# Six shared 8 KB places for transposed x and streamed weight blocks

## The chip, the core and the metric

The kernel runs on one core of one Trainium2 chip. The metric is the time of one execution on the device in microseconds (us). In three timed runs the kernel before took 891.34, 892.9 and 893.55 us, so its median is 892.9 us. All data are 32-bit floats. "PE" is the matrix engine, "DVE" the vector engine, "ACT" the scalar engine, "POOL" the GpSimd engine, and "SP" the sync engine, which here only issues DMA transfers.

## The reference

The reference is linear attention without a softmax, followed by a two-layer network with a squared ReLU:

```python
kv = np.einsum('bhsd,bhse->bhde', k, v)            # batch 8, heads 8, sequence 576, head 64
out = np.einsum('bhsd,bhde->bhse', q, kv)
rms = np.sqrt(np.mean(out * out, axis=-1, keepdims=True) + 1e-06)
attn = out / rms * g_norm
x = attn.transpose(0, 2, 1, 3).reshape(B * S, H * D)   # 4608 tokens x 512
h = x @ w_in                                        # 512 x 2048
g = np.maximum(h, 0.0) ** 2
result = g @ w_out                                  # 2048 x 512
```

## The kernel before, in words

The 4608 tokens are cut into nine strips of 512. For each strip the kernel first does the "up" product with w_in, then the "down" product with w_out. Both use a fast scheme of the Strassen kind: a product of 2 x 2 blocks is made of seven products p = 1 to 7 and of sums before and after. The down product of strips 1 to 8 applies it at two levels ("deep"), the up product does so from strip 2 on. So a strip's deep down stage has seven products p, in the order 4, 1, 2, 6, 5, 7, 3 (`DEEP_ORDER`, k = 0 to 6), and each of them has seven small products j. Product p is done in two halves, i = 0 with j = 1, 2, 3 and i = 1 with j = 4, 5, 6, 7. One small product is four 32-bit matmuls of 128 x 128 by 128 x 128, which the trace shows as eight records.

The weights of the deep stages don't all stay on the chip. They are summed once in strips 0 and 1, written to DRAM (`w_deep`, `w_in_deep`, `w_out`) and streamed back in every strip as blocks: each half product needs one, of 768 KB for i = 0 and 1 MB for i = 1, and each up product of a deep strip one of 768 KB. `stream()` (line 921) asks for the next block of a fixed list: it takes a place of 8 KB per partition from the pool `stream`, which has four, and lets SP issue the load. A place is free again when the last matmul that reads its block is done. From strip 2 on every call follows directly on the work that frees a place, so that four blocks are held or in flight at all times.

The same pool also lends places in strips 0 and 1 to the sums that are written to DRAM: `w_t` in `store_deep_sums` (line 951; `reserve`, line 918, takes the place earlier) and `w_i` in `deep_sums_in` (line 1146). The transposed x of a strip, `xT`, fills another 8 KB. It has a pool of its own with two places (line 86), one for the strip at work and one for the next, whose four tiles of 128 tokens arrive one after the other. Tiles of strip 0, of strip 1 and the first of strip 2 (tile 8) are transposed on PE and copied into place by ACT (`features`, line 627). All others are transposed in squares by DVE, written to DRAM (`send_x`, line 646) and fetched back by four transfers of 64 KB each (`fetch_x`, line 651). A fetch is due some units of a clock of steps after the send: 18 units for strip 2, 6 for later strips, where a step of strip 1 counts 2.2 in the up stage and 3.2 in the down stage.

The order of the work is written out by hand: within each engine instructions run in the order in which the program emits them. SP is one such queue. When a load waits for a place or for data, everything behind it waits too: x tiles, queries, keys, values, and stores of results. Attention is a list of `slices`, of which the main loop (line 298) puts a few between the steps of a strip. In strip 1 that list starts with the last odd tile of batch 1 and has `features` of tile 8 between the transposes T(2, 2) and T(2, 3), which DVE does.

In the down stage of strip 0 (one level, order 1, 2, 5, 6, 7, 3, 4) the loop asks for two blocks when the stage begins, for a third after p = 2 and for a fourth at its seventh step, and makes the deep sums of each block of weights soon after its product (`deep_due`, line 1402).

At the very end, product p = 3 of strip 8 is done in the second half of k = 6 in the groups of j (1), (2, 6, 5, 7) and (4, 3). After each group `together` (line 1058) does what it can of the sums on ACT and DVE into a tile `o` of 128 x 512, whose four quarters are numbered 0 to 3. The small products of p = 5 and p = 3 accumulate in the same PSUM tiles, of which there are two. The last sum adds j = 3 and j = 4 to quarters 0 and 3 together, and then `send` (line 946) stores the whole tile, 256 KB, with one transfer.

## Time and profile before

| what | value |
|---|---|
| median of three timed runs | 892.9 us |
| the profiled execution | 889.28 us |
| its span, first to last instruction | 887.3 us |
| PE busy | 876.6 us, 99% |
| PE weight loads busy | 821.8 us, 93% |
| DVE busy | 721.4 us, 81% |
| ACT busy | 352.3 us, 40% |
| POOL busy | 307.3 us, 35% |
| DMA, mean over the span | 266 GB/s |
| granted PE clock | 1.000 |

The profiled execution is one run with its own time, which is 3.6 us under the median. Its span leaves out about 2 us around the program. Durations are taken from it, so sums are made against 889.28 us. A busy engine in this profile is one that has an instruction under way. "Idle before" names the time an engine stood still before an instruction, and the arrow names what ended it. SP counts as never busy, but its own waits are listed separately.

### The profile page before, as it was taken

What the parts mean: (1) busy time and instruction counts of PE and PEld (TensorE: products, weight loads), DVE (VectorE), ACT (ScalarE), POOL (GpSimd) and SP (SyncE); (2) the same over time, 40 slices, a digit from 0 to 9 for tenths busy, and PEclk for the clock granted to TensorE, in tenths of its full rate; (3) what the DMA queues carried; (4) which work ended last, traced back from release to release, by engine and by line L of the source; (5) the groups of instructions that cost most, each with busy time, mean ns of one, the idle gap of its engine ahead of it and who ended that gap; (6) DMA issues with size and microseconds to landing.
All of it is one profiled execution on the core that took longest, in us unless ns stands there. A gap on an engine that the chain in (4) does not pass through costs nothing.

```text
span 887.3 us, 20876 instructions
## 1 busy us (share of the span) xinstructions
PE 876.6 (99%) x8296; PEld 821.8 (93%) x8296; DVE 721.4 (81%) x1233; ACT 352.3 (40%) x806; POOL 307.3 (35%) x315
## 2 busy tenths in 40 slices
PE   8999999999999999999999999999999999999998
PEld 7445888889999999999999999999999999999998
DVE  4999998879768986798678966897888778876886
ACT  4898242320048303740365034902491147102710
POOL 0000005610558223731474045604470447044700
PEclk9999999999999999999999999999999999999999
DMA  9998997989999888979887988898658864884385
GB/s 314 315 316 251 304 366 234 273 305 328 327 232 262 297 309 249 237 269 331 238 222 250 321 268 247 251 307 285 211 166 309 297 181 171 309 291 155 137 313 180
DMA packets 169953, 235.73 MB, mean 266 GB/s; under 512 B 79488, under 2 KB 134272, under 8 KB 161536
## 3 DMA queue, kind: packets, MB, share of 16 engines
q1 hardware_dynamic: 169696, 234.40, 82.3%
q8 instruction: 65, 1.06, 0.5%
q14 instruction: 32, 0.26, 0.1%
q10 hardware_dynamic: 160, 0.00, 0.0%
HBM read 197.66 MB, written 36.70 MB: 264 GB/s over the span
## 4 chain that ended last, share of the span: by engine, by line
PE 82%; DVE 10%; DMA 3%; ACT 3%; issue 2%; SPq 0%; POOL 0%; DVEq 0%; POOLq 0%; ACTq 0%
PE ps_B L1052 22%; PE ps_A L1248 19%; PE ps_A L1052 16%; PE ps_B L1248 9%; PE ps_C L1248 5%; PE ps_A L835 4%; PE kv_ps L432 2%; PE x_ps L468 2%; DVE w_c L269 2%; PE ps_B L835 1%; DMA w_deep<-w_t 1%; DVE w_t L289 1%; DVE wt L289 1%; PE ps_C L835 1%; DVE w_c L263 1%
## 5 line engine op out<-in xcount | busy, mean ns | idle before, releaser
L1052 PE MATMUL ps_B<-w_blk,g_s 128*128 128x128 f32 x1024 | 126.1, 275 | 0.0
L1052 PEld LDWEIGHTS ps_B<-w_blk,g_s 128*128 128x128 f32 x1024 | 120.0, 192 | 0.1
L1248 PE MATMUL ps_A<-x_l,w_in 128*128 128x128 f32 x784 | 103.8, 275 | 0.3 <-ACT snap L1265 0.3
L1052 PE MATMUL ps_B<-w_blk,gt 128*128 128x128 f32 x768 | 97.5, 275 | 1.5 <-DMA w_blk<-w_out 1.5
L289 POOL TENSOR_TENSOR x_l<-xT 128x256 f32<-128x256 f32 x21 | 15.4, 734 | 238.6 <-PE ps_A L1052 187.9
L1248 PEld LDWEIGHTS ps_A<-x_l,w_in 128*128 128x128 f32 x784 | 95.4, 192 | 0.6 <-ACT snap L1265 0.5
L1052 PE MATMUL ps_A<-w_blk,g_s 128*128 128x128 f32 x768 | 93.6, 275 | 0.0
L1052 PEld LDWEIGHTS ps_B<-w_blk,gt 128*128 128x128 f32 x768 | 91.5, 192 | 1.7 <-DMA w_blk<-w_out 1.7
L1052 PEld LDWEIGHTS ps_A<-w_blk,g_s 128*128 128x128 f32 x768 | 89.6, 192 | 0.0
L1260 POOL TENSOR_TENSOR snap<-snap,gt 128x512 f32<-128x512 f32 x35 | 45.9, 1310 | 119.2 <-ACT snap L1265 103.7
L1265 ACT COPY snap<-ps_A 128x512 f32<-128x512 f32 x63 | 36.9, 585 | 109.5 <-PE ps_A L1248 96.2
L1198 ACT ACTIVATE gt<-gt 128x512 f32<-128x512 f32 x112 | 70.1, 626 | 12.8 <-DVE gt L1260 12.6
L1052 PE MATMUL ps_A<-w_blk,gt 128*128 128x128 f32 x576 | 72.2, 275 | 0.0
L1199 ACT ACTIVATE gt<-gt 128x512 f32<-128x512 f32 x112 | 70.7, 631 | 3.6
L1052 PEld LDWEIGHTS ps_A<-w_blk,gt 128*128 128x128 f32 x576 | 68.2, 192 | 0.0
L1067 DVE TENSOR_TENSOR o_sb<-o_sb,ps_B 128x256 f32<-128x256 f32 (+1 forms) x128 | 49.4, 386 | 19.2 <-ACT o_sb L1068 11.8
L1068 ACT COPY o_sb<-ps_A 128x128 f32<-128x128 f32 x24 | 6.4, 265 | 145.7 <-PE ps_A L1052 145.7
L1154 POOL TENSOR_TENSOR w_i<-w_in 128x512 f32<-128x512 f32 x7 | 10.7, 1524 | 148.1 <-DMA q<-in_q_dram 140.8
L289 DVE TENSOR_TENSOR gt<-gt 128x2048 f32<-128x2048 f32 (+1 forms) x29 | 59.7, 2063 | 0.0
L1260 POOL TENSOR_TENSOR gt<-gt,snap 128x512 f32<-128x512 f32 x42 | 52.4, 1277 | 17.6 <-DVE snap L1260 17.4
L1248 PE MATMUL ps_B<-x_l,w_blk 128*128 128x128 f32 x392 | 52.1, 276 | 0.0
L1248 PE MATMUL ps_A<-x_l,w_blk 128*128 128x128 f32 x392 | 51.9, 275 | 0.0
(183 smaller groups left out, 1835.0 us busy)
## 6 DMA issues: line engine op xcount, KB each, us to landing
w_blk<-w_deep SPq DMA_DIRECT2D x56, 1024.0 KB, 6.5
w_blk<-w_out SPq DMA_DIRECT2D x56, 768.0 KB, 6.0
w_blk<-w_in_deep SPq DMA_DIRECT2D x49, 768.0 KB, 5.5
raw<-in_moe_w_in_dram SPq DMA_DIRECT2D x16, 512.0 KB, 7.0
raw<-in_moe_w_out_dram SPq DMA_DIRECT2D x16, 512.0 KB, 5.8
k<-in_k_dram SPq DMA_DIRECT2D x29, 256.0 KB, 5.2
v<-in_v_dram SPq DMA_DIRECT2D x29, 256.0 KB, 5.4
x_d<-x_q SPq DMA_DIRECT2D x27, 256.0 KB, 5.4
```

The source lines that it names most:

```text
L269: yield nc.vector.scalar_tensor_tensor(out=ci, in0=high, scalar=-(2**30), in1=ci, op0=ALU.bitwise_and, op1=ALU.bitwise_or)
L289: eng.tensor_tensor(out=out, in0=a, in1=b, op=ALU.subtract)
L432: nc.tensor.matmul(ps[ts(h, D), i], lhsT=a, rhs=w, start=i == 0 and c == 0, stop=c == C, skip_group_check=True)
L468: nc.tensor.matmul(ps[half, r, i, ts(p, D)], lhsT=q[row, half], rhs=kvd[b, p][row, row], start=True, stop=True)
L835: nc.tensor.matmul(bank[BANK[p]][:, i, :], lhsT=lhsT(k), rhs=rhs(k), start=p in (1, 5, 2) and i == 0 and k == 0, stop=k == n - 1, skip_gro ...
L1052: nc.tensor.matmul(chain[c][x][:, i, :], lhsT=a[:, f, :], rhs=w[:, f, :], start=x not in opened[c] and f == 0, stop=f == FQ // 2 - 1, skip ...
L1067: add = lambda out, a, b: nc.vector.tensor_tensor(out=out, in0=a, in1=b, op=ALU.add)
L1198: nc.scalar.activation(o, o, AF.Relu)
L1199: nc.scalar.activation(o, o, AF.Square)
L1248: nc.tensor.matmul(ps[:, i, :], lhsT=w, rhs=rhs, start=j in (1, 2, 5) and i == 0, stop=True, skip_group_check=True)
L1260: add = lambda eng, out, a, b: eng.tensor_tensor(out=out, in0=a, in1=b, op=ALU.add)
L1265: nc.scalar.copy(t, ps)
```

## The change

One pool of six places holds the streamed blocks, the weight sums and the transposed x of strips 1 to 8. The x of strip 0 has a place of its own in the storage that is given back when the weights have been converted, and the new pool lies on that storage.

- `stream()` is called once more at the start of each deep down stage (k = 0, i = 0) and no longer at k = 6, i = 0. Within the stage each block is asked for one half product earlier, and the total is the same.
- In strip 0 three blocks are asked for at the start of the down stage, the fourth after p = 2, and the request at its seventh step goes. The deep sums of p = 5 come one step later, behind those of p = 6.
- Tiles of strip 2 are due for fetching 12 units after their send, not 18.
- `features` of tile 8 comes after T(2, 3), not before it.
- The last strip's p = 5 and p = 3 use three PSUM tiles: j = 3 has one for itself. The last groups of j are (1), (2, 6, 5, 7), (4), (3). Quarters 1 and 2 of the last tile are stored before j = 4 and j = 3 are added, quarter 3 after j = 4, quarter 0 after j = 3: four transfers of 64 KB, one of them issued by ACT, in place of one of 256 KB.

```diff
-    xt_pool = ctx.enter_context(tc.tile_pool(name="xt", bufs=2))
...
     conv = ExitStack()
+    xt_pool = conv.enter_context(tc.tile_pool(name="xt", bufs=1))
...
     def open_xt(s):
         if s not in xt:
-            xt[s] = xt_pool.tile([P, STRIP // SQ, NP, SQ], FP32, name="xT", tag="xT")
+            if s == 0:
+                xt[s] = xt_pool.tile([P, STRIP // SQ, NP, SQ], FP32, name="xT", tag="xT")
+            else:
+                t = stream_pool.tile([P, 4, FQ // 2, P], FP32, name="xT", tag="w_blk")
+                xt[s] = t.rearrange("p n f e -> p (n f e)").rearrange("p (a q t) -> p a q t", q=NP, t=SQ)
         return xt[s]
...
-        tiles_due.append((clock[0] + (6 if n >= DEEP_UP * NT + NT else 18), fetch_x, (n,)))
+        tiles_due.append((clock[0] + (6 if n >= DEEP_UP * NT + NT else 12), fetch_x, (n,)))
...
-    slices += [(T, (2, 2)), (features, (last[0],)), (T, (2, 3)), (K, (2, 2, 3))]
+    slices += [(T, (2, 2)), (T, (2, 3)), (features, (last[0],)), (K, (2, 2, 3))]
...
+    def send_quarter(s, th, eh, o, t, h, eng):
+        for part, at, rows in out_rows(NT * s + 2 * th):
+            if at.start <= t < at.stop:
+                eng.dma_start(
+                    out=rows[:, t - at.start, eh * DH + h * P : eh * DH + (h + 1) * P], in_=o[part, t, ts(h, P)]
+                )
...
-    LAST_PLACE = {1: (1, 0), 2: (0, 0), 6: (0, 1), 5: (0, 2), 7: (0, 3), 3: (1, 1), 4: (1, 2)}
+    LAST_PLACE = {1: (1, 0), 2: (0, 0), 6: (0, 1), 5: (0, 2), 7: (0, 3), 3: (2, 0), 4: (1, 1)}
...
-            chain[c] = [fpsum.tile([P, 4, P], FP32, name=f"ps_{c}", tag="f") for _ in range(2)]
+            n = 2 + (s == N_STRIP - 1 and p == 5)
+            chain[c] = [fpsum.tile([P, 4, P], FP32, name=f"ps_{c}", tag="f") for _ in range(n)]
...
+        if s == N_STRIP - 1 and p in (5, 3):
+            if p == 3:
+                for t, h, eng in ((0, 1, nc.sync), (1, 0, nc.scalar)):
+                    send_quarter(s, 0, 1, o, t, h, eng)
+            yield
+            for j, t, h in ((4, 1, 1), (3, 0, 0)):
+                add(q[:, 2 * t + h], q[:, 2 * t + h], small(j)[:, 0])
+                if p == 3:
+                    send_quarter(s, 0, 1, o, t, h, nc.sync)
+                    yield
+            return
...
     def down_deep(s, k, i):
         p = DEEP_ORDER[k]
+        if k == i == 0:
+            stream()
...
-            for js in ((1,), (2, 6, 5, 7), (4, 3)):
+            for js in ((1,), (2, 6, 5, 7), (4,), (3,)):
...
-        stream()
+        if k < 6:
+            stream()
...
-                stream_pool = ctx.enter_context(tc.tile_pool(name="stream", bufs=4, reuse_waits="tile"))
+                stream_pool = ctx.enter_context(tc.tile_pool(name="stream", bufs=6, reuse_waits="tile"))
...
-                stream(2)
+                stream(3)
...
-            if i == n_up + 6:
-                stream()
-            while deep_due and i not in (n_up + 1, n_up + 4, n_up + 12, n_up + 13):
-                deque(store_deep_sums(*deep_due.popleft()), 0)
+            while deep_due and i not in (n_up + 1, n_up + 4, n_up + 5, n_up + 12, n_up + 13):
+                deque(store_deep_sums(*(deep_due.pop() if i == n_up + 6 else deep_due.popleft())), 0)
```

More of the change, by code (lines that the diff above doesn't have):

```diff
@@ L946, in send @@
     def send(s, th, eh, o):
-        for i, (part, t, rows) in enumerate(out_rows(NT * s + 2 * th)):
-            eng = nc.scalar if i % 2 and s == N_STRIP - 1 and (th, eh) == (0, 1) else nc.sync
-            eng.dma_start(out=rows[:, :, ts(eh, DH)], in_=o[part, t, :])
+        for part, t, rows in out_rows(NT * s + 2 * th):
+            nc.sync.dma_start(out=rows[:, :, ts(eh, DH)], in_=o[part, t, :])
+    def send_quarter(s, th, eh, o, t, h, eng):
[4 more added lines that the diff above has]
+                )
     def store_deep_sums(p, w):
```

## The prediction, made before the change was run

> **What bounds the kernel now.** The first view is the page's share of busy time.

> ```profile
> PE 876.6 (99%) x8296; PEld 821.8 (93%) x8296; DVE 721.4 (81%) x1233; ACT 352.3 (40%) x806; POOL 307.3 (35%) x315
> ```

> PE is the bound: 876.6 of 887.3 us. The change removes no matmul, so it can only touch the 10.7 us in which PE stands still, at the start, at the end and in waits. The second view lists who PE waited for; times are in total, how often, longest.

> ```profile
> PE ps_B L1052 <- DMA w_blk<-w_out: 1.5, 1, 1.5
> ...
> PE ps_A L835 <- DVE o_sb L1001: 0.4, 1, 0.4
> PE ps_B L1248 <- DVE snap L1260: 0.4, 1, 0.4
> PE ps_A L1248 <- ACT snap L1265: 0.3, 1, 0.3
> PE xt_ps L632 <- DVE x_n L563: 0.3, 1, 0.3
> ```

> The reader is to see that a single wait is for a streamed block. The third view is SP's line in time around it, and the fourth PE's.

> ```profile
> 186.31 0.84 SPq L933 DMA_DIRECT2D w_blk<-w_out  x1
> 199.04 0.32 SPq L939 DMA_DIRECT2D w_blk<-w_deep  x1
> ...
> 199.88 5.53 SPq L655 DMA_DIRECT2D xT<-x_d  x8
> 205.45 0.43 SPq L933 DMA_DIRECT2D w_blk<-w_out  x1
> ```

> ```profile
> 192.71 1.89 PE L835 MATMUL ps_B<-xT,w_in 128*128 128x256 f32 x8
> 194.44 1.89 PE L835 MATMUL ps_A<-x_t,w_in 128*128 128x256 f32 x8
> ...
> 210.33 2.05 PE L1052 MATMUL ps_B<-w_blk,gt 128*128 128x128 f32 x16 [1.50 <-DMA w_blk<-w_out]
> ```

> The load of the fourth block of strip 1 issues at 199.04 us. SP's own waits say why it is late, and the table of stretches what that costs the transfers (the last two columns are DMA share and GB/s).

> ```profile
> SPq L939 <- PE ps_B L1052: 11.3, 1, 11.3
> ```

> ```profile
> 196.00:199.00 3.00, 3.00 (x28) 2.97 (x27) 2.97 (x5) 1.23 (x2) 0.00 (x0) 1.00 0.19 73
> ```

> SP held the queue for 11.3 us until the first deep half product gave back its place; the DMA engines fell to 19%. Then eight x fetches went ahead of the fifth block (205.45), which landed at 210.28, when PE had needed it 1.5 us before. The landings that follow are close too: in the trace the next blocks of that stage land 0.4 to 2.6 us before their first matmul, in strip 2's down stage 0.7 to 4.7 us.

> **The change part by part.**

> *Lookahead in strip 1.* The fourth block needs a place. The x of strip 1 has its last reader in the matmuls at 192.71, over at 194.44, and its place is now in the pool: SP's block ends at about 194.5, 4.5 us sooner. Even if the x fetches keep their 5.53 us ahead of the fifth block, it issues near 194.5 + 0.4 + 5.5 = 200.4 and, with the 4.8 us it took before, lands at 205.2; PE needs it at 208.8. Gone: 1.5 us. The earlier due time (12 units of 2.2 a step, 2.7 steps sooner) moves fetches ahead of the blocks too, but into the 11.3 us in which SP stood still. Late next is the sixth block (0.36 us ahead of its use before); it moves one half product, 2.7 or 3.6 us, forward with the rest. DVE, which could be late next, ends its sums for that product at 214.25 and waits for PE after, so it doesn't take the gain back.

> *Lookahead in later strips.* The call at k = 0 takes the place of the strip's own x, the call left out at k = 6 leaves one for the x after next. While two x tiles are alive four places remain, as before; so POOL's sums of strip 1, which take places too and wait 7.3 us for a store once, find what they found, and POOL's next reader of them is past 230. No PE wait on a block stands in the profiled execution there, so in its sum this is worth nothing; the cover is the landing margins above. In a run with slower transfers it is worth what they then cost.

> *Strip 0's down stage.* Views of SP, ACT and DVE there:

> ```profile
> 101.23 0.81 SPq L930 DMA_DIRECT2D w_blk<-w_out  x2
> 104.89 2.85 SPq L965 DMA_DIRECT2D w_deep<-w_t  x2
> ...
> 112.66 2.39 SPq L930 DMA_DIRECT2D w_blk<-w_out  x1
> ```

> ```profile
> 104.64 1.07 ACT L633 COPY xT<-xt_ps 128x512 f32<-128x512 f32 x2 [4.95 <-PE xt_ps L632]
> ```

> ```profile
> 128.59 0.69 DVE L289 TENSOR_TENSOR w_t<-w_blk 128x512 f32<-128x512 f32 x1 [0.46 <-DMA w_deep<-w_t]
> ```

> The third block moves from 112.66 to about 102.1. Its 1 MB goes ahead of the two 1 MB stores of 104.89 and 107.4, which landed at 112.58 and 115.05; at the 319 GB/s of the stretch from 100 to 120 us they land 3.3 us later. Places then: three blocks, two sums, and at 104.64 the x of strip 1 as the sixth. The fourth block is the seventh: SP waits for the first store, till about 115.6. Queued behind it are a store of results, two keys and two values (115.1 to 117.3 before), first used at 145: covered by 25 us. The block itself issues some 5 us sooner than its 120.68. The sums of p = 5 (115.48 before) would need a place at that moment; they now stand behind those of p = 6, four DVE instructions of 0.69, so at 118.1, when the second store lands: 0 to 0.5 us. The 0.46 us that DVE waited at 128.59 goes, as a block's place is free by then. DVE is 96% busy there and PE waited 0.42 for it at 131.87: minus 0.4 us.

> *Tile 8 of strip 2.* Its PE transposes waited 0.29 us for DVE at 155.62. One slice later, about 0.9 of a step of 1.7 us, this goes: minus 0.3. In exchange DVE meets T(2, 3) sooner, whose query landed at 161.95 with DVE ready at 162.03; moved ahead of two instructions of together 1.8 us, DVE can stand up to 1.8 us, with two sums for PE behind it. PE is one step (1.7 us) away from needing them. Bounds 0 and 1.8; I take 0.2, near the lower end, since DVE has free time of 2 us at 163.4.

> *The last tile.* After the group (2, 6, 5, 7) DVE works without a stop:

> ```profile
> 881.78 1.20 DVE L1067 TENSOR_TENSOR o_sb<-o_sb,ps_B 128x256 f32<-128x256 f32 x3 [2.15 <-PE ps_B L1052]
> 883.01 0.69 DVE L1067 TENSOR_TENSOR o_sb<-o_sb 128x512 f32<-128x512 f32 x1
> 883.80 0.42 DVE L1067 TENSOR_TENSOR o_sb<-o_sb,ps_B 128x256 f32<-128x256 f32 x1
> ```

> PE's last matmul (883.2) isn't what DVE waits for, so splitting (4, 3) frees nothing. The add of 0.42 becomes two of 0.29, done at 884.09 and 884.42 in place of 884.22. SP issues quarter 1 at 883.8, quarter 3 at 884.2 and quarter 0 at 884.6, at 0.37 us each as for the last store; ACT has quarter 2. The 256 KB store took 2.15 us from issue (884.30) to landing (886.45); the fastest 64 KB fetches took 1.82 to 2.0. Quarter 0 so lands between 886.4 and 886.75: minus 0.05 to plus 0.3, I take plus 0.1. The third PSUM tile is free since DVE's reads for p = 2 end at 860.60, while p = 5 starts at 864.40; the extra add falls into 1.3 us in which DVE waited for ACT (876.55).

> [...]

> **Sum** on the profiled execution: 1.5 + 0.4 + 0.3 gained, 0.2 + 0.1 lost: minus 1.9 us, 889.28 to 887.4. The median shown is 3.6 us above that execution. What makes timed runs longer isn't traced; the thinnest thing in the trace is the margin of landings (0.05 to 1.5 us for 14 blocks of strips 1 and 2), and lookahead widens just that. I put a third of the 3.6 us, 1.2, down to it. From the median: 892.9 - 1.9 - 1.2 = 889.8 us, 0.35% faster.

> **The rivals.**

> 1. *Only what the trace shows.* The 3.6 us have another cause, or T(2, 3) costs 1 us more: a gain of 1 to 2 us, 891.3, within 0.3% (2.7 us, about what a measurement of this kernel can tell from no change). For it: 99% PE, one DMA wait. Against it: six margins under 1 us.
> 2. *All of the 3.6 us are late blocks.* Then 892.9 - 1.9 - 3.6 = 887.4. For it: the stages of strips 1 and 2 run at 85 to 93% DMA share. Against it: no wait of this kind after 210 us.
> 3. *Slower: the x of strip 1 finds no place.* If the fourth block's load takes the sixth place before 104.64, ACT stands at that copy until the first store lands, 115.6: 11 us. Behind it are the copies that PE's products need (108.5) and the squares that DVE's next 4 us hang on. PE goes on to 116.5; ACT then needs 1.07 + 0.59 + 1.08 + 0.6 us to catch up, DVE, 96% busy, doesn't: 5 us lost, net plus 3.1, 896.0. It decides from about 4.6 us of ACT wait on. Against it: SP stands behind the second sum, done only at 107.40.

> **How the numbers follow.** The forecast 0.40 (888.5 to 890.6), rival 1 0.29, rival 2 0.17, rival 3 0.14. Faster by over 0.3% means under 890.2: rival 2 and nearly all of the forecast, 0.55; slower, over 895.6: 0.14; the same 0.31. The range leaves out rival 3 and the lower edge of rival 2: 887.0 to 893.4, whose upper part is rival 1 with the upper bounds of T(2, 3) and the tail.

> **What would show it.** Right: no PE wait on w_blk at about 209; SP's wait before the fourth block of strip 1 down from 11.3 to about 7; DMA share over 0.5 just ahead of the deep stage; blocks landing 3 us or more ahead from k = 1 on; no DVE wait near 128. Wrong: ACT waiting at line 633 or its successor for a store of w_t; DVE idle over 1 us at T(2, 3); a PE wait on w_in_deep blocks or x tiles in strips 2 and later; a last landing past 886.75 minus what was gained.

## The result, and the profile after

The changed kernel takes 896.05 us in the median of 18 runs, and the kernel before 892.79 us in 18 runs beside it. The ratio is 1.0032, with a 95% interval of 1.0019 to 1.0045, so the change made the kernel slower, by 0.3%. Predicted was 889.8 us. Times are medians; of the ten runs of the second experiment below one took 2258.28 us and is left out of its ratio, and one took 898.21 us at a granted clock of 0.949 and is in it. The profiled execution after took 895.67 us with a span of 893.8 us, 6.5 us more than the span before.

First the share of busy time and the granted clock from the page of the changed kernel.

```profile
PE 878.1 (98%) x8296; PEld 822.9 (92%) x8296; DVE 720.1 (81%) x1235; ACT 352.3 (39%) x806; POOL 307.6 (34%) x315
...
PEclk9999989999999999999999999999999999999999
```

PE has the same 8296 instructions, is busy for 1.5 us longer and stands still for 5 us longer. The clock row has one lower digit, in the sixth of 40 slices (112 to 134 us). So the loss is at one place. The list of waits of the changed kernel between 96 and 140 us shows who waited there (in total, how often, longest).

```profile
ACT xT L637 <- DMA w_deep<-w_t: 18.2, 1, 18.2
DVE ms L485 <- ACT sq L477: 8.4, 1, 8.4
...
PE xt_ps L636 <- DVE x_n L563: 5.5, 1, 5.5
```

The lines read from top to bottom as a chain. ACT stands at the copy of x for a *store* of `w_t`, DVE stands for ACT's squares, and PE stands for the x_n that DVE makes of them. The lines of SP, ACT and PE follow, each in order of time.

```profile
101.96 1.28 SPq L934 DMA_DIRECT2D w_blk<-w_out  x3
104.87 2.85 SPq L975 DMA_DIRECT2D w_deep<-w_t  x2
107.76 8.55 SPq L330 DMA_DIRECT2D w_out<-w_in  x2
116.36 3.79 SPq L934 DMA_DIRECT2D w_blk<-w_out  x1
```

```profile
117.84 1.07 ACT L637 COPY xT<-xt_ps 128x512 f32<-128x512 f32 x2 [18.19 <-DMA w_deep<-w_t]
118.81 0.60 ACT L849 COPY snap<-ps_B 128x512 f32<-128x512 f32 x1
119.28 1.12 ACT L477 ACTIVATE sq<-x_ps 128x512 f32<-128x512 f32 x2
```

```profile
110.88 7.17 PE L839 MATMUL ps_A<-w_blk,gt 128*128 128x256 f32 x32
123.54 1.94 PE L636 MATMUL xt_ps<-ident,x_n 128*128 128x128 f32 x8 [5.49 <-DVE x_n L563]
125.27 8.47 PE L839 MATMUL ps_A<-w_blk,gt 128*128 128x256 f32 x32
```

The store issued at 104.87 landed at 117.75 us, and ACT started its copy at 117.84. So the x of strip 1 was given the place of the first weight sum, and had to wait until that sum was in DRAM. The place that the prediction had meant for x went to the fourth block, as the compiled program shows: the load goes to the one place that nothing had used before. (The place that the same step reserves for the sum of p = 5 is that of the second sum.) SP issued the load only at 116.36 us, 10 us after x needed a place. The place was taken where the program *asks* for the block, not when the load leaves.

The PE line shows a second cost. The same 32 records take 8.47 us behind the stop and 7.17 ahead of it, although nothing is waited for. The table of stretches says why: its columns are the bounds, the length, busy time and instructions of PE, PEld, DVE, ACT and POOL, and then the granted clock.

```profile
118.05:121.40 3.35, 0.00 (x1) 0.00 (x0) 1.42 (x3) 2.35 (x5) 0.00 (x0) 0.98 1.00 279
121.40:123.54 2.14, 0.00 (x1) 0.03 (x1) 1.65 (x7) 2.08 (x3) 0.00 (x0) 0.50 0.87 279
123.54:128.10 4.56, 4.56 (x15) 4.02 (x16) 4.49 (x8) 3.68 (x5) 0.00 (x0) 0.50 1.01 358
128.10:133.50 5.40, 5.40 (x26) 4.75 (x26) 5.33 (x7) 3.69 (x2) 0.00 (x0) 1.00 1.04 395
```

Some 3.2 us after PE's last matmul (at 121.27 by the trace's clock records) the granted clock fell to 0.50, and it came back at 128.09, 4.6 us after PE had begun again. PE thus worked for 4.6 us at half speed. The traces of this case have four stops of this kind (this one, its repeat, and below the runs with 20 and with 24 copies on ACT), of 5.5, 4.0, 6.0 and 11.0 us. In this order, the fall came 3.2, 2.3, 3.2 and 5.0 us after PE's last matmul, the clock stayed at 0.50 for 6.82 us three times and for 10.24 us the fourth time, and it returned 4.6, 5.2, 4.0 and 4.3 us after PE had begun again.

Matching the matmuls of the two traces one by one gives the balance (the changed kernel's start minus that of before):

| at, in the trace before | behind by | what happened in between |
|---|---|---|
| 109.5 us | 1.4 us | arises at 51 to 55 us, raw weights landing later (see the last runs below) |
| 116.5 us | 7.0 us | PE's wait for x_n |
| 119.0 us | 9.2 us | half speed |
| 132.2 us | 8.5 us | DVE's wait of 0.46 us is gone |
| 156 to 158 us | 7.6 to 8.0 us | the wait at tile 8's transposes is gone, and more |
| 210.3 us | 6.4 us | the wait for w_blk is gone |
| end of PE | 6.2 us | nothing |
| end of the span | 6.5 us | the tail |

So most of the gains that were predicted are there, and 7.8 us (from 1.4 to 9.2) were lost at one place, by the mechanism that the prediction had priced as its third rival.

### The profile page after: what moved, and what is told of

Same layout as the page of the kernel before. It is cut to its first block, busy times and chain, and to the rows that moved or that the text cites. A ratio compares the mean times of both kernels' runs of the same rounds, so it can differ in the third digit from the quotient of the medians.

```text
span 893.8 us, 20892 instructions
## 1 busy us (share of the span) xinstructions
PE 878.1 (98%) x8296; PEld 822.9 (92%) x8296; DVE 720.1 (81%) x1235; ACT 352.3 (39%) x806; POOL 307.6 (34%) x315
## 4 chain that ended last, share of the span: by engine, by line
PE 84%; DVE 6%; ACT 5%; DMA 4%; issue 1%; SPq 0%; DVEq 0%; ACTq 0%
PE ps_B L1063 22%; PE ps_A L1273 18%; PE ps_A L1063 17%; PE ps_B L1273 9%; PE ps_A L839 5%; PE ps_C L1273 5%; PE ps_B L839 2%; PE kv_ps L432 2%; DMA raw<-in_moe_w_in_dram 2%; PE x_ps L468 2%; DMA w_deep<-w_t 1%; DVE w_c L269 1%; ACT raw L254 1%; ACT w_c L251 1%; PE ps_C L839 1%
## 5 line engine op out<-in xcount | busy, mean ns | idle before, releaser
L289 POOL TENSOR_TENSOR x_l<-xT 128x256 f32<-128x256 f32 x21 | 15.8, 750 | 236.9 <-PE ps_A L1063 236.9
L1223 ACT ACTIVATE gt<-gt 128x512 f32<-128x512 f32 x112 | 70.1, 626 | 12.8 <-DVE gt L1285 12.7
L1078 DVE TENSOR_TENSOR o_sb<-o_sb,ps_B 128x256 f32<-128x256 f32 (+1 forms) x130 | 49.6, 383 | 19.4 <-ACT o_sb L1079 11.8
L289 DVE TENSOR_TENSOR gt<-gt 128x2048 f32<-128x2048 f32 (+1 forms) x29 | 59.7, 2063 | 0.0
```

The costliest lines, as they stand in the source:

```text
L289: eng.tensor_tensor(out=out, in0=a, in1=b, op=ALU.subtract)
L1078: add = lambda out, a, b: nc.vector.tensor_tensor(out=out, in0=a, in1=b, op=ALU.add)
L1223: nc.scalar.activation(o, o, AF.Relu)
```

## The experiments

Two theories. **A:** the place that the fourth block took is the whole cause. **B:** blocks asked for further ahead fill the DMA queue, and the loss comes from the transfers. A third, **C**, says that the lookahead brings nothing and only the accident at 105 us differs.

### The fourth block asked for after x

```diff
-        if p not in (1, 7) and (s, p) not in ((0, 5), (0, 6), (0, 3), (0, 4)):
+        if p not in (1, 7) and (s, p) not in ((0, 2), (0, 6), (0, 3), (0, 4)):
             stream()
```

> The changed kernel, with one request moved: the fourth streamed block of strip 0 is asked for after the p = 5 product instead of after the p = 2 product, and so after the x of strip 1 has taken its place. Theory A (the place that the fourth block's request took is the whole cause of the loss): ACT's wait of 18.2 us at the copy of x for a store of w_t and PE's wait of 5.5 us for x_n are gone, the eight half-speed microseconds of matmuls after it too; with about 7.5 us less than the changed kernel's median the time is 888.5 us, under before's by 0.4%. Rival B (blocks asked for further ahead keep the queue full, and the loss is in the transfers): the wait at the copy goes, but the time stays above 893.5. Rival C (lookahead is worth nothing, only the accident goes): 891.5 to 893, as before.

Measured: 888.79 us against 893.13 for before, ratio 0.9956 (0.9941 to 0.9972). Against the changed kernel the instructions of PE, DVE, ACT and POOL stand in the same order; on SP one load moved behind one store of results and four loads of keys and values. ACT's line in this kernel:

```profile
105.77 1.07 ACT L637 COPY xT<-xt_ps 128x512 f32<-128x512 f32 x2 [5.30 <-PE xt_ps L636]
```

The copy waits for PE's transposes and for nothing else; the clock is 1.000, and PE has no wait over 0.3 us between 96 and 260 us. Theory A holds, and B falls: all the other requests are as far ahead as in the changed kernel. C falls as it was priced (891.5 to 893 us); what the lookahead by itself is worth is asked further below. (The expectation speaks of eight half-speed microseconds; the table above has 4.6.)

### Strip 0's requests as before

```diff
-                stream(3)
+                stream(2)
...
+            if i == n_up + 6:
+                stream()
-            while deep_due and i not in (n_up + 1, n_up + 4, n_up + 5, n_up + 12, n_up + 13):
-                deque(store_deep_sums(*(deep_due.pop() if i == n_up + 6 else deep_due.popleft())), 0)
+            while deep_due and i not in (n_up + 1, n_up + 4, n_up + 12, n_up + 13):
+                deque(store_deep_sums(*deep_due.popleft()), 0)
```

> The changed kernel, with the requests and sums of strip 0's down stage in the order they had before (two blocks at its start, the third after p = 2, the fourth two steps later, the sums in order of arrival); the pool of six, the lookahead of later strips, the due time, the order of the slices and the tail stay changed. Theory A: no wait of ACT for a store of w_t, since the x of strip 1 finds a place that nothing used; 888 to 890 us, within 0.15% of the kernel that only moves the fourth block. Rival B: as the changed kernel, 894 or more. If the earlier third block is worth something by itself, this one is 0.5 to 1 us slower than the one that only moves the fourth block.

Measured: 889.45 us, ratio 0.9967 (0.9945 to 0.9988). ACT copies at 105.41 after waiting for PE alone. Another way to give x its place has the same effect. The difference of 0.7 us to the kernel above is within what these runs can tell, so an earlier third block has no shown worth.

### The end as before

The kernel of the first experiment with the two PSUM tiles, the groups (1), (2, 6, 5, 7), (4, 3) and the stores of the kernel before:

```diff
-            for js in ((1,), (2, 6, 5, 7), (4,), (3,)):
+            for js in ((1,), (2, 6, 5, 7), (4, 3)):
```

> The kernel with the fourth block asked for after x, and the end of the last tile as it was before: two PSUM tiles, products 4 and 3 together, one add, two stores instead of four. Theory: the quarters cost 0.35 us at the end of the trace (from PE's last matmul to the end 4.18 us in the changed kernel, 3.83 before), so this one is 0.2 to 0.5 us faster than the other, about 888.1. Rival: the four smaller stores are worth something or nothing: the same or slower by up to 0.3 us; PE's end to the span's end stays 4.0 us or more.

Measured: 889.37 us, ratio 0.9958 (0.9943 to 0.9973), not to be told from 888.79. The theory of 0.35 us falls, as the traces explain. With quarters the last transfer lands 3.26 us after the start of the last 128x512 add, with the whole tile 3.40 here and 3.44 before. But from PE's end to the end of the span the traces have 3.83 us (four of before) and 4.10 (this one) with the old end, 3.90 (four kernels) and 4.18 (the rest) with the new. A step of 0.28 us comes with either end. It lies behind the last landing, in the program's closing semaphores: POOL's last two are 0.07 us apart in the trace before and 0.37 in the first experiment's. Like with like, the quarters cost 0.07 us. The last landing comes 0.14 to 0.18 us sooner with them: from issue to landing 256 KB took 2.12 to 2.15 us, and 64 KB took 1.58 to 1.71 us from SP and 1.85 to 1.86 from ACT.

### What a hold of ACT costs by itself

This kernel, and every variant after it, is the kernel of the first experiment with one more edit.

```diff
         ps = apsum.tile([P, NP, P], FP32, name="xt_ps", tag="at")
...
+        for _ in range(24 if n == NT else 0):
+            nc.scalar.copy(ps, ps)
...
```

> The kernel with the fourth block asked for after x, and 24 copies of a PSUM tile onto itself (about 0.55 us each, 13 us together) on ACT just ahead of the copy of the first x tile of strip 1: it measures by itself what it costs when ACT is held at that place for as long as the store held it (in the changed kernel from about 104.6, when the transposes were done, to 117.8 us). Theory A: it costs what the changed kernel lost there, PE waits 4.5 to 6.5 us for x_n and runs at half rate for about 2 us after it, 6.5 to 8.5 us over the kernel without the copies, 895 to 897. Rival: the hold of ACT is covered, and the changed kernel's wait of PE had another cause (the third block's transfer ahead of the stores, say): under 2 us.

Measured: 900.39 us, 11.6 us over the kernel without the copies. This trial missed its place. Tiles 6 and 7 are copied first and tile 4 comes 14 us later, at 119.27 us. There DVE stood 9.7 us for ACT's scaling of `w_in` and PE stood 11.0 us for DVE: of 14.4 us of hold only 3.4 are covered at that spot. The next run has the hold where it belongs, `range(20 if n == NT + 2 else 0)`.

> The same trial with the hold of ACT at its right place: the copies that waited in the changed kernel are those of tiles 6 and 7, which come first, and the 24 copies of the last trial stood ahead of tile 4, 14 us later. Now 20 copies of the PSUM tile onto itself, 0.6 us each by that run, 12 us together, ahead of the copy of tile 6 at about 105; the fourth block is asked for after x, so nothing else is late. Theory A: what the changed kernel lost there comes back without its cause: ACT free at about 117, PE waits 4.5 to 6.5 us for x_n at the same place and runs slowly for some us after it, 6 to 8.5 us over the 888.8 of the kernel without copies, 895 to 897. Rival (ACT's hold is covered, the third block's transfer ahead of the stores made PE wait): under 2 us, 891 or less.

Measured: 895.35 us, ratio 1.0030 to before, 6.6 us over the first experiment's 888.79 and 5.4 over the 889.92 of its repeat, below. The changed kernel is 7.3 and 6.1 us over the same two. The waits of this kernel between 96 and 145 us, and ACT's line:

```profile
DVE ms L485 <- ACT sq L477: 8.3, 1, 8.3
...
PE xt_ps L636 <- DVE x_n L563: 6.0, 1, 6.0
```

```profile
106.89 12.00 ACT L638 COPY xt_ps<-xt_ps 128x512 f32<-128x512 f32 x20 [6.08 <-PE xt_ps L636]
```

They are the two lines of the changed kernel again, without any store in them, and the clock was 0.50 from 121.83 to 128.65 us. Matched with the first experiment's trace, PE loses 6.2 us up to the first matmul behind the wait and 1.9 in slow matmuls. This is the loss of the changed kernel, made by nothing but a hold of ACT. Of 12.0 us of hold, 6.0 are covered. The half, `range(10 if n == NT + 2 else 0)`, asks whether that cover is a fixed time:

> The hold of ACT ahead of the copy of tile 6 halved, 10 copies, 6 us. In the run with 20 copies 12.0 us of hold gave 6.0 us of PE wait, so that 6.0 us were covered; if the cover is a fixed time, 6 us cost PE 0 to 0.3 us, no slow matmuls follow, and the time is within 0.7 us of the kernel without copies. If the hold costs half of what the full one did, 3.3 us.

Measured: 890.23 us, where the kernel without copies took 889.92 beside it. ACT was held for 5.99 us, no wait of PE for x_n follows, and the clock is 0.999. Both holds fit a fixed cover of 6 us.

### What is worth what, from strip 1 on

```diff
-        if k == i == 0:
-            stream()
...
-        if k < 6:
-            stream()
+        stream()
```

> The kernel with the fourth block asked for after x, and without the request further ahead in the strips from 1 on (no request at k = 0, one again at k = 6): six places, blocks asked for as before. If the lookahead is what gains, the PE wait for w_blk near 209 us is back in part (0.5 to 1.5 us), the landing margins fall back to 0 to 2 us and the time is 1.5 to 3.5 us over the 888.8, 890.3 to 892.3. If the place of x that comes free at the end of strip 1's up products gains by itself, under 1 us.

Measured: 890.41 us, ratio 0.9971 (0.9959 to 0.9984), against 0.9956 (0.9941 to 0.9972). So the two were run once more side by side.

> The kernel with the fourth block asked for after x once more, as the measure for the three beside it: 888 to 889.7 us, faster than before by 0.35 to 0.55%.

> The kernel without the request further ahead from strip 1 on, beside the one that has it, on one chip: 1.0 to 2.0 us slower if the lookahead by itself is worth what the traces show from strip 1 on (late blocks at the start of the deep stages), within 0.5 us if the first comparison was a matter of its chip and runs.

Measured: 889.92 us with the lookahead and 890.61 without, both 0.9974 of before's 892.57. The request one half product earlier is worth 0.7 to 1.6 us by the medians and isn't shown by the intervals. The waits of PE for blocks, below, agree with a small gain. Without the lookahead the kernel is still 0.26 to 0.29% faster than before. Putting back strip 0's requests, the end, the due time or the order of the slices (the runs above and below) costs nothing that shows either. That leaves the two more places, by elimination; no run shows it.

> The kernel with the fourth block asked for after x, and the x fetches of strip 2 due after 18 units again instead of 12. In the kernel with 12 the eight fetches stand between two block loads at 188 to 198 us, each issue released only by the landing of the transfer issued eight before it, and hold SP for 10 us; the block behind them lands 0.5 us ahead of its use. With 18 they should come behind that block: it issues at 195 or sooner, its margin is over 3 us, no other block's falls under 0.3 us. In time, 0 to 1 us faster than 888.8 if late blocks cost anything in ordinary runs; the same within 0.5 us if not.

```diff
-        tiles_due.append((clock[0] + (6 if n >= DEEP_UP * NT + NT else 12), fetch_x, (n,)))
+        tiles_due.append((clock[0] + (6 if n >= DEEP_UP * NT + NT else 18), fetch_x, (n,)))
```

Measured: 889.76 us, ratio 0.9962 (0.9948 to 0.9976), the same. The first of its lines in time of SP is the changed kernel, the second this one; the eight fetches stand once ahead of the fourth block of strip 1 (line 943) and once behind it.

```profile
194.23 0.71 SPq L937 DMA_DIRECT2D w_blk<-w_out  x1
196.48 11.16 SPq L659 DMA_DIRECT2D xT<-x_d  x8
207.74 0.38 SPq L943 DMA_DIRECT2D w_blk<-w_deep  x1
```

```profile
196.45 0.32 SPq L943 DMA_DIRECT2D w_blk<-w_deep  x1
196.87 0.38 SPq L652 DMA_DIRECT2D x_d<-x_q  x1
197.30 8.66 SPq L659 DMA_DIRECT2D xT<-x_d  x8
206.06 0.38 SPq L937 DMA_DIRECT2D w_blk<-w_out  x1
```

The expectation is met for one block and missed for the next. The fourth lands 1.8 us ahead of its use and not 0.5, and now the fifth has no margin. Either way SP is held 9 to 11 us by eight issues of 0.3 us. The traces show transfers with eight landing semaphores in turn, and none of SP's issues behind its first eight (662 in the kernel before, 664 in the changed one) starts ahead of the landing of the transfer that SP issued eight before it. In the changed kernel each of the eight starts within 0.02 us of the landing of the transfer issued eight before it: the first at 196.48, when the block issued at 188.96 landed at 196.46, the last at 207.33, when the block of 194.23 landed at 207.32. In both orders the transfer behind them has the thin margin (0.10 us for the fourth block in the changed kernel).

```diff
-    slices += [(T, (2, 2)), (T, (2, 3)), (features, (last[0],)), (K, (2, 2, 3))]
+    slices += [(T, (2, 2)), (features, (last[0],)), (T, (2, 3)), (K, (2, 2, 3))]
```

> The kernel with the fourth block asked for after x, and the order of the two slices as before (tile 8's features ahead of the last transposed query of batch 2). By the trace the new order saves PE's 0.3 us at tile 8's transposes and makes DVE wait 3.3 us for that query, of which PE sees 0.2: no difference, within 0.4 us. Rival: DVE's wait costs as much as 1.8 us further on, then this one is 1 us or more faster.

Measured: 889.49 us, ratio 0.9966 (0.9955 to 0.9978), beside 889.92: no difference, as expected. DVE waits 0.97 us for the query in this order, 3.31 in the other (first experiment) and 0.66 in the changed kernel; PE sees next to nothing of either.

### The kernel before, and the changed one, profiled again

> The kernel before, profiled once more: its profiled execution lay 3.6 us under its median, and the prediction put 1.2 of it down to blocks that come late. If late blocks make its ordinary runs longer, the trace of a run at 892 or more has further PE waits for w_blk, of 1 us or more together, in the down stages of strips 1 and 2. If something at its start does, the time up to the deep stages is longer and the waits are the same.

Measured: 892.61 us, near the median. PE's waits of that run between 200 and 260 us:

```profile
PE ps_B L1052 <- DMA w_blk<-w_out: 1.8, 2, 1.6
PE ps_B L1052 <- DMA w_blk<-w_deep: 1.7, 1, 1.7
```

The execution behind the prediction had 1.5 us in a single such wait. Matched with it, this run falls behind by 0.4 us at 132 us, by 0.1 at 210, by 2.7 more between 231 and 239 us, at blocks that land as they are needed, and by 0.2 at 500 us: 3.3 in all. Late blocks are most of what made this ordinary run longer.

> The kernel before, profiled a third time, for its first 110 us: in the two traces so far the first product with a streamed block starts at 109.51 and 109.57 us, in the twelve of changed kernels at 109.67 to 111.96. If the start-up loads merely vary, it is over 110 in one or both of these two runs; if the places of the new pool slow the start, both are under 109.8. Late blocks: 1 to 4 us of PE waits for w_blk, as in the other two.

> The kernel before, profiled a fourth time, the same: over 110 us for the first product with a streamed block if start-up loads merely vary, under 109.8 if the places of the new pool slow the start; 1 to 4 us of PE waits for w_blk.

> The changed kernel, profiled once more. ACT's wait at the copy of x for the store of w_t comes again, 17 to 19 us, PE's wait for x_n of 5 to 6.5 us behind it, and a granted clock of about 0.5 for some 2 us. If the 1.3 us by which the first trace was behind at 55 us is a matter of the run, it is anything from 0 to 2.4 us here; if it is the change's, over 0.5 again.

In this order: 890.22, 890.20 and 894.60 us. The changed kernel shows its chain again, each link 1 us shorter than the least expected: ACT 16.0 us for the store, PE 4.0 us for x_n, and a clock of 0.50 behind it. The kernel before waited 2.1 and 3.1 us for blocks. In the profiles of before and of the kernels with and without the lookahead:

| kernel | PE's waits for w_blk, us |
|---|---|
| before (four runs) | 1.5, 3.5, 2.1, 3.1 |
| six places, old lookahead (two) | 0.9, 0.8 |
| six places, new lookahead (the changed kernel twice, the first experiment, its repeat) | 0, 0.3, 0, 0.9 |

In the second experiment's kernel it is 0.5 us; the others have no such wait over 0.3 us.

As to the start-up: the first product with a streamed block begins at 109.51, 109.57, 110.12 and 110.04 us in the four runs of before, at 110.88 and 110.53 in the changed kernel, and at 109.67 to 111.96 in eleven runs of its variants. The start varies by itself, since two runs of before are over 110 and two variants under 109.8. Whether the new addresses add something to it (the means are 109.8 and 110.8) stays open.

## Why the prediction was wrong, point by point

- **Strip 0's down stage, the places.** Here it failed. The step said "at 104.64 the x of strip 1 as the sixth. The fourth block is the seventh". It is the other way round. The request for the fourth block stands in the step of p = 2, ahead of the slice that copies x, and `stream()` lends the place there. That SP reaches the load only at 116.36 doesn't matter for who gets it. This is the third rival, and the evidence that the prediction held against it ("SP stands behind the second sum, done only at 107.40") speaks of the load, not of the place.
- **The rival's price.** It said 11 us of ACT, 5 us of PE, a cover of 4.6 us and 896.0 us. Measured are 11.8 us of ACT (from 106.0, when the transposes were done by the first experiment's line and its offset of 0.2 us), 5.5 us of PE, a cover of 6 us, 2.2 us of half speed that it didn't have, and 896.05. The gains were larger than in its sum, too (from 9.2 us behind to 6.2, for 1.9), so the agreement of the last number is partly luck.
- **The third block ahead of the stores.** Estimated to delay the first store by 3.3 us; it landed at 117.75 for 112.58, 5.2 us later. That term lengthened the hold: a store landing where it did before would have held ACT for 6.6 us, about what is covered. By this estimate the two edits of strip 0 harm each other; no run has the early fourth request without the early third block.
- **The wait for w_blk at 210 us, 1.5 us.** Right: gone, and the balance moves by 1.7 us between 158 and 210 us. But not by the path described. SP's block was to end at 194.5 and the fourth block to go sooner. Its place did come free, and then the fetches, due earlier, stood ahead of it for 11.2 us, since each had to await the landing eight issues back. The fourth block's margin was 0.10 us (0.74 before). The fifth gained, from 0.05 to 1.17, because no fetches stood ahead of *it* any more. SP's hold before the fourth block was to fall from 11.3 to about 7 us; it is 12.8 from the last issue.
- **Blocks 3 us or more ahead from k = 1 on.** Wrong in strip 1 (0.1 to 3.9 us) and at two blocks of strip 2 (2.1 and 2.3 us); right in later strips, as in the deep stage at 680 to 710 us: 4.8 to 7.0 us, where before had 1.2 to 4.3. The share of the DMA engines just ahead of the deep stage was to exceed 0.5. It is 1.01 in the last 5 us ahead of it, but it was so before, too (191 to 196 us), so this sign tells nothing: the stretch with 0.19 is the stage's own first 3 us, where the changed kernel has 0.72 (204.2 to 207) and the first experiment 0.83.
- **A third of the 3.6 us for late blocks, 1.2.** The size is about so; that the request further ahead is what brings it isn't shown, since the kernels without it wait only 0.8 to 0.9 us. With the 1.5 us of the sum, 2.7 us were put down to blocks; the four profiles of before have 2.6 us of such waits on average, and the changed kernel and its first variant 0.3. The whole of the 3.6 us (rival 2) isn't it.
- **0.4 at 131.87 and 0.3 at tile 8.** Both waits are gone in the changed kernel, and the balance moves by 0.7 us and by 0.5 to 0.9. The first gain is no constant: four runs of the variants without ACT's long hold have 1.0 to 1.3 us of wait at that product, two runs of before none.
- **T(2, 3), 0.2 lost.** Right: DVE waits 0.7 to 3.3 us, PE 0.2 at most. The reading behind it had DVE ready after the query landed; in that trace DVE already stood 0.29 us for this query, so there was no slack.
- **The tail, 0.1.** Right in size, 0.07. The working was off in both halves: the quarters land 0.14 to 0.18 us sooner, where the prediction took 0.1 later, and the closing semaphores are what varies.

With the one request moved, the kernel ran at 888.79 and 889.92 us, on both sides of the 889.8 forecast. What failed was a single step: the order in which the fourth block and the x of strip 1 get their places. This version is faster than before by 0.44% and 0.26% in its two comparisons, and by the ratios to before 0.6 to 0.8% faster than the changed kernel: it beats both.

## What to carry to other kernels

When tiles of different kinds come to share one pool, work out who gets which place from the order in which the program asks for them, and not from the time at which a load or copy will run; a request far ahead takes a place at once, though its queue reaches it 10 us after the other tile needs it. Ask then what the loser gets, and who must let go of it: here a store that waits behind 3 MB of loads. When a hold of a side engine is priced, find its cover (6 us here, 3.4 us at a spot 14 us later) and add the slow matmuls that follow when the clock has fallen (a stop of PE of 4.0 us was enough here; one of 1.9 us, in the fourth run of before with a mean granted clock of 1.000, was not).
